# x by way of a bf16 copy in DRAM, one h matmul ahead at accumulator swaps, new round counts: a fused convolution and ELU layer on one core

## The chip, the cores and the metric

One core of a Trainium2 chip. The metric is the device time of one execution in microseconds. The kernel before took 740.35 us (median of 3 runs, 740.33 to 741.36). Every run also comes with the span of its core and the mean granted TensorE clock.

## The reference

A softmax-weighted causal convolution over 7 tokens (8 heads of 24 channels), then two matrix products with an ELU between them:

```python
def _attn_ref(x, weight):                 # x: 8 x 4096 x 192, weight: 8 x 7
    w = exp(weight - max(weight, -1)); w = w / (sum(w, -1) + 1e-09)
    x_pad = concatenate([zeros((B, 6, D)), x], axis=1)
    # ... windows of 7 tokens, one weight row per head
    return einsum('hk,bskhg->bshg', w, x_unf).reshape(B, S, D)

def _moe_ref(x, w_in, w_out):             # 32768 x 192, 192 x 2048, 2048 x 192
    h = x @ w_in
    g = np.where(h > 0.0, h, exp(np.minimum(h, 0.0)) - 1.0)
    return g @ w_out
```

## The kernel before

The tokens go in 32 supers of 1024 tokens, each super in 16 slots of 128 hidden features. TensorE is used as two row tiles of 64 partitions, each with 512 of a super's tokens for h. One h matmul chain (three of 512 columns) fills one of six PSUM banks. ACT takes exp of it, POOL clamps, DVE makes the ELU from both; then the bank is free. The products g times w_out of the super before are spread over the slots by `ROUNDS`. An accumulator is filled by one tile first and by the other afterwards, and each such swap is a semaphore wait. The next super's convolution also runs on PE. Its order against the rest comes from a modelled start time of each operation:

```python
LAG = -4
ROUNDS = (
    ((0, (0, 17)), (1, (6, 4, 7, 11, 4)), (0, (15,))),
    ((0, (0, 14, 8, 10)), (1, (4, 10, 5, 13))),
)
CONV_AT = ((2, 1, 1, 0), (8, 1, 1, 1), (12, 2, 0, 0), (15, 2, 0, 1))
EARLY_CONV = ((6, 1, 0, 0), (7, 1, 0, 1), (8, 1, 1, 0), (9, 1, 1, 1), (11, 2, 0, 0), (12, 2, 0, 1))
M_NS, R_NS, C_NS = 216, 83, 236
X_AT = ((3, 2, 1), (8, 2, 0), (11, 3, 2))
X_LATE = (17, 3, 2)
# ...
    # the schedule: one list of operations per row tile, merged by a modelled start time
    steps = []
    tiles, at = ([], []), [0, 0]

    def put(rt, ops_of):
        cost = {"h": M_NS, "o": R_NS, "c": C_NS, "w": M_NS}
        for op in ops_of:
            tiles[rt].append((at[rt], rt, len(tiles[rt]), op))
            at[rt] += cost[op[0]]
    for n in range(NP):
        s, i = divmod(n, NQ)
        convs = [(ahead, g, b) for at, ahead, g, b in EARLY_CONV if at == n]
        convs += [
            (s + ahead, g, b)
            for at, ahead, g, b in CONV_AT
            if at == i and s + ahead < NS
            and (s + ahead, g, b) not in [e[1:] for e in EARLY_CONV]
        ]
        for u in range(2):
            rt = 1 - u
            beside = [("c", 2 * cs + g - 2, b, u) for cs, g, b in convs]
            if n < first_round:
                beside += [("w", rt)] * WARM[1]
            beside += [single(item, rt) for item in rounds_at.get(n, ())]
            put(u, [("h", n, u, j) for j in range(3)])
            put(rt, beside)
        if n % 2:
            at[:] = [max(at)] * 2
    steps.extend(op for *_, op in sorted(tiles[0] + tiles[1], key=lambda v: v[:3]))
# ...  POOL: x by two casting DMAs a super, clamps
            def load_x(s, part):
                # ...
                src = bass.AP(
                    tensor=x_flat.tensor,
                    offset=row * D,
                    ap=[[D, P], [TOK * D, whole], [1, D]],
                )
                g.dma_start(xg[:, b, v0 : v0 + whole, :], src).then_inc(s_x[b][part - 1], 16)
                for at, ahead, part in X_AT:
                    if at == i and s and s + ahead < NS:
                        load_x(s + ahead, part)
                if n == X_LATE[0]:
                    load_x(*X_LATE[1:])
                for u in range(2):
                    W(s_exp, 2 * n + u + 1)
                    g.tensor_scalar(
                        out=E[:, n % NE, u, :],
                        in0=E[:, n % NE, u, :],
                        scalar1=1.0,
                        scalar2=0.0,
                        op0=ALU.min,
                        op1=ALU.max,
                    ).then_inc(s_clp)
# ...  DVE: the convolution's weights reversed, then the ELUs
            W(s_band, 48)
            v.tensor_copy(Tm[:], Tr[:, :, ::-1]).then_inc(s_tm)
                    W(s_clp, 2 * n + u + 1)
                    v.scalar_tensor_tensor(
                        out=gT[:, s % NG3, q, u, :],
                        in0=E[:, n % NE, u, :],
                        scalar=1.0,
                        in1=bank_of(op[:3]),
                        op0=ALU.subtract,
                        op1=ALU.max,
                    ).then_inc(s_tt)
# ...  PE: a chunk of h, and a product
                elif op[0] == "h":
                    _, n, r, j = op
                    s, q = divmod(n, NQ)
                    if n == 0:
                        W(s_ha, 2)
                        W(s_hd, 2)
                    if j == 0:
                        if Q_PART[q] < 3:
                            W(s_w[Q_PART[q]], 32)
                        else:
                            W(s_wc, 16)
                        W(s_att[s % 2], 16 * ((s + 1) // 2))
                        wait_bank()
                    ins = pe.matmul(
                        bank_of(op[:3]),
                        w_in[
                            HP * r : HP * (r + 1),
                            j,
                            2 * FC * (q // 2) + q % 2 : 2 * FC * (q // 2 + 1) : 2,
                        ],
                        att[HP * r : HP * (r + 1), s % 2, j, 0:GS],
                        start=(j == 0),
                        stop=(j == 2),
                        tile_position=(HP * r, 0),
                    )
                    if j == 2:
                        ins.then_inc(s_h[r])
                else:
                    # ...
                    W(s_tt, 2 * (NQ * t + q) + g + 1)
                    at_end = acc[:2] == (last, 1)
                    if x_ in begins:
                        if at_end:
                            wait_bank()
                        elif acc in previous:
                            taken(W, previous[acc])
                    elif steps[seen[acc]][2] != rt:
                        W(s_swap[1 - rt], ends_run[seen[acc]])
                    to = bank_of(("l",) + acc) if at_end else ops[:, g, :]
                    d0 = 0 if at_end else D * kb
                    t0 = 2 * P * half + P * kb
                    ins = pe.matmul(
                        to[:, d0 : d0 + D],
                        gT[HP * rt : HP * (rt + 1), t % NG3, q, g, t0 : t0 + P],
                        w_out[HP * rt : HP * (rt + 1), q, :],
                        start=(x_ in begins),
                        stop=(x_ in stops),
                        tile_position=(HP * rt, 0),
                    )
                    if x_ in ends_run:
                        ins.then_inc(s_swap[rt])
```

At the start, the first super's convolution runs as matmuls against diagonal weights (the head), into `att`. The weights of the later convolutions pass through DRAM (`conv_taps`), land in `Tr`, and the DVE copy shown above turns them into `Tm`. Filler matmuls on zeros (`WARM`) keep PE at work while there are no products.

## Time and profile before

| kernel before | us |
|---|---|
| median of 3 runs | 740.35 |
| span of the traced run | 739.3 |
| start to the first h of super 1 | 34.4 |
| one steady super | 22.36 |

The prediction below shows the profile's lines. They are read in this way. The first line of the page says how full each engine is. The windows table gives busy time over one super. The waits view says which instruction waited for which, how long in all, how often, and the longest time. A timeline line has the start and the length in us, engine, line, operation and what it writes and reads, how many in a row, and in brackets the idle time before it and what ended that.

### The profile page before, as it was taken

The numbers are of one execution on the slowest core, as the hardware profiler recorded it, in microseconds if no ns is written. First come the engines' busy times: TensorE is split into PE (matmuls) and PEld (weight loads), VectorE is DVE, ScalarE is ACT, GpSimd is POOL, SyncE is SP. The second block draws the span as 40 slices with busy tenths as digits, with TensorE's granted clock in tenths as the row PEclk, the third lists the DMA queues.
The fourth block names the chain that finished last, engine by engine and source line by source line (L and its number), as shares of the span: only waits on it lengthen the run. The fifth ranks groups of instructions, "written<-read, shape, count | busy, mean of one in ns | idle before, by whom it ended". The sixth has DMA issues, their size and how long they took to land.

```text
span 739.3 us, 28636 instructions
## 1 busy us (share of the span) xinstructions
PE 730.8 (99%) x11878; PEld 648.1 (88%) x11878; DVE 649.3 (88%) x1044; ACT 665.9 (90%) x1286; POOL 666.7 (90%) x1108
## 2 busy tenths in 40 slices
PE   8999999999999999999999999999999999999998
PEld 4589889999889999889899899998899998888987
DVE  4889889889889889889898898898898898898995
ACT  5889999999999999999999999999999999999984
POOL 7899999999999999999999999999999999998884
PEclk9999999999999999999999999999999999999999
DMA  9553444634434534546534435434445344343212
GB/s 171 93 95 74 72 78 77 96 73 79 74 65 91 94 71 69 88 60 96 89 67 71 88 67 95 80 75 71 77 79 95 72 80 75 72 82 82 56 36 67
DMA packets 131862, 58.97 MB, mean 80 GB/s; under 512 B 96020, under 2 KB 131348, under 8 KB 131732
## 3 DMA queue, kind: packets, MB, share of 16 engines
q0 software_dynamic: 43136, 17.28, 22.5%
q1 hardware_dynamic: 88308, 39.37, 20.8%
q8 instruction: 93, 1.52, 0.9%
q10 hardware_dynamic: 288, 0.49, 0.2%
q14 instruction: 37, 0.30, 0.1%
HBM read 35.61 MB, written 25.17 MB: 82 GB/s over the span
## 4 chain that ended last, share of the span: by engine, by line
PE 95%; DVE 2%; POOL 1%; ACT 1%; DMA 1%; issue 0%; SPq 0%; ACTq 0%
PE ops L759 49%; PE H L727 42%; PE H L703 2%; DVE gT L588 2%; POOL E L447 1%; PE H L759 1%; ACT E L519 1%; DMA xf<-in_x_dram 1%; PE H L660 0%; PE ops L660 0%; PE H L640 0%; DVE xh L554 0%; ACT csb L497 0%; POOL xg L397 0%; PE H L628 0%
## 5 line engine op out<-in xcount | busy, mean ns | idle before, releaser
L588 DVE SCALAR_TENSOR_TENSOR gT<-E,H 128x512 f16<-128x512 f32 x1024 | 642.6, 683 | 74.4 <-POOL E L447 69.0
L447 POOL TENSOR_SCALAR E<-E 128x512 f32<-128x512 f32 x1024 | 606.8, 614 | 60.9 <-ACT E L519 50.4
L727 PE MATMUL H<-att,w_in 64*128 64x512 bf16 x3072 | 626.2, 376 | 1.4 <-DVE gT L588 0.6
L519 ACT ACTIVATE E<-H 128x512 f32<-128x512 f32 x1024 | 573.4, 605 | 52.0 <-PE H L727 42.0
L759 PE MATMUL ops<-w_out,gT 64*128 64x192 f16 x8064 | 619.1, 243 | 0.6
L759 PEld LDWEIGHTS ops<-w_out,gT 64*128 64x128 f16 x8064 | 537.1, 94 | 41.0 <-PE ops L759 24.9
L727 PEld LDWEIGHTS H<-att,w_in 64*128 64x128 bf16 x3072 | 259.1, 94 | 29.0 <-DVE gT L588 7.9
L703 PE MATMUL H<-xg,Tm 64*128 64x240 bf16 x496 | 90.7, 263 | 0.9 <-DVE gT L588 0.9
L497 ACT ACTIVATE csb<-H 128x480 bf16<-128x480 f32 x124 | 71.3, 575 | 0.0
L489 ACT ACTIVATE osb<-ops 128x384 f32<-128x384 f32 x125 | 61.0, 488 | 10.2 <-PE ops L759 5.9
L397 POOL DMA_DIRECT2D xg<-in_x_dram x62 | 55.0, 888 | 0.1
L703 PEld LDWEIGHTS H<-xg,Tm 64*128 64x128 bf16 x496 | 43.4, 94 | 11.2 <-issue 1.1
L677 PE MATMUL ops<-zw 64*128 64x512 bf16 x24 | 8.8, 377 | 0.0
L759 PE MATMUL H<-w_out,gT 64*128 64x192 f16 x128 | 6.6, 243 | 0.0
L759 PEld LDWEIGHTS H<-w_out,gT 64*128 64x128 f16 x128 | 6.0, 94 | 0.0
L616 PE MATMUL ops<-zw 128*128 128x512 bf16 x9 | 4.0, 631 | 1.3 <-DVE zw L529 1.3
L402 POOL DMA_DIRECT2D w_in<-in_moe_w_in_dram x7 | 4.6, 662 | 0.3 <-DMA wh<-in_weight_dram 0.3
L580 DVE COPY osb<-ops 128x384 f32<-128x384 f32 x1 | 0.6, 557 | 4.5 <-PE ops L759 4.5
L616 PEld LDWEIGHTS ops<-zw 128*128 128x128 bf16 x9 | 1.2, 142 | 3.2 <-issue 1.9
L565 DVE CAST att<-H 128x512 bf16<-128x512 f32 x1 | 0.7, 693 | 2.3 <-PE H L660 2.3
L677 PEld LDWEIGHTS ops<-zw 64*128 64x128 bf16 x24 | 2.3, 94 | 0.5
L554 DVE CAST xh<-xf 128x768 bf16<-128x768 f32 x1 | 1.0, 995 | 1.9 <-DMA xf<-in_x_dram 1.9
(46 smaller groups left out, 26.2 us busy)
## 6 DMA issues: line engine op xcount, KB each, us to landing
out_dram<-osb SPq DMA_DIRECT2D x126, 192.0 KB, 3.7
xg<-in_x_dram POOLq DMA_DIRECT2D x61, 240.0 KB, 5.2
w_in<-in_moe_w_in_dram POOLq DMA_DIRECT2D x4, 192.0 KB, 6.2
w_out<-in_moe_w_out_dram POOLq DMA_DIRECT2D x1, 768.0 KB, 15.0
att<-csb SPq DMA_TRANSPOSE x31, 3.5
xf<-in_x_dram ACTq DMA_DIRECT2D x1, 384.0 KB, 3.1
xf<-in_x_dram SPq DMA_DIRECT2D x1, 384.0 KB, 4.2
w_in<-in_moe_w_in_dram POOLq DMA_DIRECT2D x1, 288.0 KB, 10.3
```

The lines of the kernel that those rows point to most:

```text
L397: g.dma_start(xg[:, b, v0 : v0 + whole, :], src).then_inc(s_x[b][part - 1], 16)
L402: g.dma_start(w_in[HP * r : HP * (r + 1), :, c0:c1], moe_w_in.rearrange("(p j) f -> p j f", j=3)[:, :, c0:c1],).then_inc(s_w[k], 16)
L447: g.tensor_scalar(out=E[:, n % NE, u, :], in0=E[:, n % NE, u, :], scalar1=1.0, scalar2=0.0, op0=ALU.min, op1=ALU.max,).then_inc(s_clp)
L489: a.activation(*out_pieces(acc), ACT.Copy).then_inc(s_oev)
L497: return a.activation(csb[:, s % 2, :].rearrange("p (j v h i) -> p h j v i", j=3, v=2 * WPG, h=HEADS)[:, h0 : h0 + HB], bank_of(("c", m, b ...
L519: a.activation(E[:, n % NE, u, :], bank_of(op[:3]), ACT.Exp).then_inc(s_exp)
L588: v.scalar_tensor_tensor(out=gT[:, s % NG3, q, u, :], in0=E[:, n % NE, u, :], scalar=1.0, in1=bank_of(op[:3]), op0=ALU.subtract, op1=ALU.m ...
L616: pe.matmul(ops[:, 0, :], zw[:, 0:P], zw[:], start=True, stop=True)
L677: pe.matmul(ops[:, rt, :], zw[HP * rt : HP * (rt + 1), 0:P], zw[HP * rt : HP * (rt + 1), :], start=True, stop=True, tile_position=(HP * rt ...
L703: ins = pe.matmul(bank_of(op[:3])[:, n1 * hh : n1 * (hh + 1)], Tm[HP * rt : HP * (rt + 1), h, :], xg[HP * rt : HP * (rt + 1), s % NXB, :, ...
L727: ins = pe.matmul(bank_of(op[:3]), w_in[HP * r : HP * (r + 1), j, 2 * FC * (q // 2) + q % 2 : 2 * FC * (q // 2 + 1) : 2,], att[HP * r : HP ...
L759: ins = pe.matmul(to[:, d0 : d0 + D], gT[HP * rt : HP * (rt + 1), t % NG3, q, g, t0 : t0 + P], w_out[HP * rt : HP * (rt + 1), q, :], start ...
```

## The change

The intent is threefold. PE should not idle at the three swaps of a super: the first h of the slot goes ahead of the product that must wait. POOL should have fewer DMAs to issue: it casts a whole super of x into a DRAM copy with one DMA, and SyncE loads from there. And the head should let the first h start sooner. The counts of products per slot, the slots of the convolution, and its order (now by single chunks) change with it. So does a load of w_in: POOL now issues both halves of the last piece (8 issues in place of 7), where SyncE copied the second half from the first. Core of the diff, cuts marked by "...", three comments added:

```diff
-    ((0, (0, 17)), (1, (6, 4, 7, 11, 4)), (0, (15,))),
-    ((0, (0, 14, 8, 10)), (1, (4, 10, 5, 13))),
+    ((0, (0, 20)), (1, (1, 7, 9, 7, 8)), (0, (12,))),
+    ((0, (0, 15, 7, 10)), (1, (5, 8, 6, 13))),
...
-CONV_AT = ((2, 1, 1, 0), (8, 1, 1, 1), (12, 2, 0, 0), (15, 2, 0, 1))
+CONV_AT = ((4, 1, 1, 0), (10, 1, 1, 1), (12, 2, 0, 0), (15, 2, 0, 1))
...
-M_NS, R_NS, C_NS = 216, 83, 236
+M_NS, R_NS, C_NS = 215.8, 82.5, 102.5
...
-X_AT = ((3, 2, 1), (8, 2, 0), (11, 3, 2))
-X_LATE = (17, 3, 2)
+X_PAD, X_COPY, X_LOAD = 8, 1, 15
+X_LATE = (13, 22)
...
+    turns_at = {
+        n
+        for n, items in rounds_at.items()
+        if items
+        and rounds_at.get(n - 1)
+        and rounds_at[n - 1][-1][:2] == items[0][:2]
+        and rounds_at[n - 1][-1][4] != items[0][4]
+    }
...
-            beside = [("c", 2 * cs + g - 2, b, u) for cs, g, b in convs]
+            beside = [
+                ("c", 2 * cs + g - 2, b, u, hh)
+                for cs, g, b in convs
+                for hh in range(HB)
+            ]
...
-            put(u, [("h", n, u, j) for j in range(3)])
+            if rt and n in turns_at:
+                beside.insert(0, ("h", n, 1, 0))
+            put(u, [("h", n, u, j) for j in range(u and n in turns_at, 3)])
...
+    xb = nc.dram_tensor("x_cast", (NT, D), BF16).ap()
...
-            return H[:, (0, 2, 0)[j], GS * r : GS * r + GS // 2]
+            return H[:, (0, 2, 1)[j], GS * r : GS * r + GS // 2]
...
+            def copy_x(s):                                   # POOL, in slot X_COPY
+                W(s_cv, 4 * (s - NXB - 1) + 1)
...
+                g.dma_start(
+                    xb[s * SUP : (s + 1) * SUP, :].rearrange("(p t) d -> p (t d)", p=P),
+                    x_flat[s * SUP : (s + 1) * SUP, :].rearrange("(p t) d -> p (t d)", p=P),
+                ).then_inc(s_xb[s % 2], 16)
...
             W(s_xha, 1)                                      # PE, the halo matmuls
-            W(s_xh, 1)
...
             ins.then_inc(s_tp)
+            W(s_xh, 1)
...
                     if n == 0:
-                        W(s_ha, 2)
-                        W(s_hd, 2)
+                        W(s_ha, (1, 1, 2)[j])
+                        W(s_hd, (0, 1, 2)[j])
...
+            def load_cast(s):                                # SyncE, in slot X_LOAD
+                W(s_cv, 4 * (s - NXB))
+                W(s_xb[s % 2], 16 * ((s - 1) // 2 + (s % 2)))
...
+                for part in range(2):
+                    row = s * SUP + GS * part - PAD
+                    for w0, w1, rows in ((0, WPG - 1, P), (WPG - 1, WPG, GS - TOK * (WPG - 1) + PAD)):
+                        v0 = WPG * part
+                        sy.dma_start(
+                            xg[0:rows, s % NXB, v0 + w0 : v0 + w1, :],
+                            bass.AP(tensor=xb.tensor, ...),
+                        ).then_inc(s_xq[s % NXB][part], 16)
```

## The prediction

> **What bounds the kernel now.** Some names first. A super is 1024 tokens (32 of them), a slot is one of its 16 chunks of 128 hidden features. In a slot each of the two row tiles of TensorE (partitions 0-63 and 64-127) does three h matmuls (x times w_in, 512 columns), then or before them a number of products (g times w_out, 192 columns), and in four slots of a super two chunks of the next convolution (240 columns). h goes through ACT (exp), POOL (clamp) and DVE (ELU) before its PSUM bank is free; six banks rotate. I read the page first, for the engine that is full.
>
> ```profile
> PE 730.8 (99%) x11878; PEld 648.1 (88%) x11878; DVE 649.3 (88%) x1044; ACT 665.9 (90%) x1286; POOL 666.7 (90%) x1108
> ...
> L588 DVE SCALAR_TENSOR_TENSOR gT<-E,H 128x512 f16<-128x512 f32 x1024 | 642.6, 683 | 74.4 <-POOL E L447 69.0
> L447 POOL TENSOR_SCALAR E<-E 128x512 f32<-128x512 f32 x1024 | 606.8, 614 | 60.9 <-ACT E L519 50.4
> L727 PE MATMUL H<-att,w_in 64*128 64x512 bf16 x3072 | 626.2, 376 | 1.4 <-DVE gT L588 0.6
> ...
> L759 PE MATMUL ops<-w_out,gT 64*128 64x192 f16 x8064 | 619.1, 243 | 0.6
> L759 PEld LDWEIGHTS ops<-w_out,gT 64*128 64x128 f16 x8064 | 537.1, 94 | 41.0 <-PE ops L759 24.9
> ...
> L703 PE MATMUL H<-xg,Tm 64*128 64x240 bf16 x496 | 90.7, 263 | 0.9 <-DVE gT L588 0.9
> ```
>
> Everything is near 90%, PE is at 99%, and the chain that ended last is 95% PE. But busy PE hides a tile that idles beside the other. So next I matched the trace's matmuls to the two tiles in program order. Starts that follow each other on one tile are 216 ns apart for h, 82.5 for a product and 102.5 for a convolution chunk. Per super and tile that is 48 x 216 + 128 x 82.5 + 8 x 102.5 = 21.75 us. The starts of successive supers are 22.36 us apart (the two table rows below, over one super each), so each tile idles 0.61 us per super, some 19 us in all. That, and the start, is all there is to win on PE.
>
> ```profile
> core 0: us, PE busy (x) PEld busy (x) DVE busy (x) ACT busy (x) POOL busy (x), PEclk, DMA share, GB/s
> 392.75:415.11 22.36, 22.34 (x373) 20.20 (x369) 20.06 (x33) 20.72 (x41) 20.62 (x35) 1.00 0.43 79
> 415.11:437.47 22.36, 22.34 (x372) 20.22 (x370) 20.15 (x33) 20.72 (x41) 20.79 (x36) 1.00 0.43 79
> ```
>
> The view of waits, and PE's timeline at one of them, say where it lies:
>
> ```profile
> PEld ops L759 <- PE ops L759: 24.9, 94, 0.5
> ```
> ```profile
> 412.42 0.38 PE L727 MATMUL H<-att,w_in 64*128 64x512 bf16 x1
> 412.44 0.24 PE L759 MATMUL ops<-w_out,gT 64*128 64x192 f16 x1
> 412.52 0.39 PE L727 MATMUL H<-att,w_in 64*128 64x512 bf16 x1
> 412.90 0.25 PE L759 MATMUL ops<-w_out,gT 64*128 64x192 f16 x1
> 412.91 0.39 PE L727 MATMUL H<-att,w_in 64*128 64x512 bf16 x1
> ```
>
> 94 is three per super for 31 supers and one more: the swaps, where an accumulator passes from one tile to the other. At 412.42 tile 1 streams its last h (until 412.64), at 412.44 tile 0 its last product. Tile 1's next product, on tile 0's accumulator, starts at 412.90: 263 ns after its h. Tile 0's second h, behind it in the queue, starts at 412.91, 175 ns late. In a steady super I find 263 twice, and 58 at the third swap, where two convolution chunks (205 ns) stand ahead: 263 - 205 = 58. With some 12 ns behind each, tile 1's 0.61 us is complete. Tile 0 loses as much: twice 185, 141 on an eviction at the first product of half 1, and 80.
>
> **What the Trainium skill says.** "TensorE: Matmul & The Clock Gate", Part 3, has matmuls in strict program order at start and end, with only weight loads pulled ahead. The trace agrees: tile 0's free h waits behind tile 1's blocked product, and all swaps are released at the same distance from the h before (its 376 ns end plus about 100), even where tile 0's product had finished earlier. "DMA: Bandwidth & Descriptors", SWDGE vs HWDGE vs iDMA, says that a casting DMA must come from GpSimd; so the cast stays there and only the plain load can go to SyncE. "Perfetto Trace Analysis", DMA Instruction — SWDGE (GPSIMD), says that such a row is descriptor generation, not movement; here it holds POOL for 0.89 us while landing takes 5.2, and POOL's clamps wait behind it:
>
> ```profile
> 398.00 0.61 POOL L447 TENSOR_SCALAR E<-E 128x512 f32<-128x512 f32 x1 [0.28 <-ACT E L519]
> 398.56 0.89 POOL L397 DMA_DIRECT2D xg<-in_x_dram  x1
> 399.49 3.02 POOL L447 TENSOR_SCALAR E<-E 128x512 f32<-128x512 f32 x5
> ```
>
> **The change part by part.**
> *An h ahead at swaps.* The matmul put ahead covers 216 of 263 ns, so 47 remain. Swaps one and two gain 216 each, the third (convolutions are moved off it) 58 - 47 = 11. That is 443 ns per super, x 31 + 216 = 13.95 us. Tile 0 is no longer blocked, as its second h is issued before the product.
> *Convolution from slots 2 and 8 to 4 and 10.* Slot 4 has no products; it grows from 648 to 853 ns, so the first product of half 1 on tile 0 comes 1501 ns after the accumulator's end instead of 1296. The 141 ns wait needed 1437 and goes. It lay beside tile 1's losses, so I add nothing.
> *Head.* The halo matmuls stop waiting for DVE's cast of the second half (they started at 6.57; the ACT half was done at 4.81), some 0.4 us. The first h waits only for the first piece of att; the third starts when att's last piece is there, 0.43 us sooner. Together 0.8 us. The start is then a chain of ACT, POOL and DVE, which shifts as a whole:
>
> ```profile
> 12.19 0.38 ACT L484 ACTIVATE att<-H 128x256 bf16<-128x256 f32 x1 [1.16 <-PE H L660]
> ...
> 12.72 0.37 PE L727 MATMUL H<-att,w_in 64*128 64x512 bf16 x1 [0.57 <-ACT att L484]
> ```
>
> *x by way of DRAM.* POOL issues one DMA per super instead of two of 0.89 us. The w_in loads (192 runs) held it 0.63 us, x (640 runs) 0.89; a copy of 128 rows I estimate from these at 0.62, with the step to the next clamp 0.65. POOL was never the bound, so the 1.1 us saved per super is worth nothing by itself, except where it ended a wait: about 0.4 us near 656, where a pad, a remainder load and x stood together. SyncE's loads have from slot 15 to slot 12 of the next super, 18 us; x landed in 5. Hidden, as is the doubled traffic at a DMA share of 0.43.
> *Finer convolution order, exact durations.* Ordering only: 0.
>
> Sum: 740.35 - 13.95 - 0.8 - 0.4 = 725.2 us, if nothing else becomes the wait.
>
> **The rivals.**
> *First: the copy in slot 1 delays a bank.* From the end of an h to the reuse of its bank, an undisturbed chain takes 197 (to exp) + 678 (to clamp) + 646 (to ELU) + 683 (its time) + 58 = 2262 ns; spacings in a queue are 494 on ACT, 576 on POOL, 605 on DVE. These I checked on the 398 us event above, where they give each start within 10 ns. In the new counts slots 1, 2 and 3 take 1225, 1308 and 1638 + 59. From the start of slot 1: the last clamp of slot 0 starts at about 0.95, the copy at 1.51, and the clamps of (1,0), (1,1), (2,0) at 2.16, 2.73, 3.31 us. The ELUs follow at 2.80, 3.41, 4.01, the last ends at 4.70 and frees its bank at 4.76. Tile 1's h of slot 4, six bank turns later because the convolution now takes one there, wants it at 1225 + 1308 + 1697 + 205 = 4.435. So PE would wait 0.3 us in each of 28 supers, 8.4 us. Without the copy the bank is free 0.3 before. For it: the arithmetic, and that a DMA row blocks POOL. Against it: in the kernel before, both loads stand just before long slots (15 and 13 products), and the tightest bank turns have 58 to 70 ns, which is no wait; whoever set these counts did so on such waits, and would hardly accept a new one where a later slot was free.
> *Second: short slots 14 and 15.* Slot 15's end comes 789 + 1430 = 2219 ns after the last h of slot 13, whose bank the first h of the next super takes after 2262: about 45 ns, x 30 = 1.4 us.
> *Third: another engine becomes the bound.* Per super: DVE 32 x 605 = 19.4 us, POOL 32 x 576 + 0.65 = 19.1, ACT 32 x 494 + 4 x 450 + 4 x 370 = 19.1. All lie under 21.75, so no.
> *Fourth: the loads come late or disturb the transposes of att*, now started two slots later. About 6 us remain from the convolution's eviction to the next super; landings took 3.4 to 5.1. Not expected.
>
> **Range and chances.** With both stalls in full: 725.2 + 8.4 + 1.4 = 735.0. Without: 725.2. I give the stall 60%, as the arithmetic fits the old trace but the design speaks against it: 0.6 x 735.0 + 0.4 x 725.2 = 731.1, so 731. Eight times in ten between 724.5 and 737.5. Over 2% faster means below 725.5: only with no stall and nothing else lost, 0.17. Slower by 2%: 0.01. Within 2%: 0.82.
>
> **What would show it right or wrong.** PEld's wait for products should fall from 24.9 us to under 10, with the product one h and about 47 ns behind. Successive supers should start 21.95 us apart without the stall, 22.25 with it; the stall would show as PE waiting for DVE at the second tile's h of slot 4, right after POOL's copy. The first h should start near 11.9 us, the first exp near 12.75. I am wrong if POOL's copy is much shorter than 0.6 us, if the swaps keep their 263, if PE waits on x or att, or if the start is held by a weight load.

## The result, and the profile after

| | before | after |
|---|---|---|
| median of 4 runs, us | 740.45 | 738.83 |
| lowest to highest | 740.33 to 741.36 | 736.52 to 738.92 |
| first h of super 1 (traced run) | 34.39 | 34.65 |
| supers 1 to 30, together | 671.32 | 666.79 |
| one steady super | 22.36 | 22.25 |
| last part | 33.59 | 32.76 |

The ratio is 0.9968, with a 95% interval of 0.9947 to 0.9989: the same within 2%. A ratio here is always the mean time of one kernel's fast runs over that of the other's in the same rounds, so it is not quite the ratio of the medians. 738.83 lies above the predicted range of 724.5 to 737.5.

One thing must be seen first. Of the four runs, the traced one had 736.52 us (span 734.2, clock 1.000), and the three others 738.81 to 738.92 (spans 736.4 to 736.5, clock 0.998). The trace shows the quicker kind.

From the page after: the engines, and POOL's copies.

```profile
PE 726.9 (99%) x11878; PEld 653.8 (89%) x11878; DVE 655.4 (89%) x1044; ACT 675.9 (92%) x1286; POOL 637.4 (87%) x1080
...
L410 POOL DMA_DIRECT2D x_cast<-in_x_dram x29 | 15.4, 530 | 0.0
```

PE is still at 99%. POOL lost 29 us of work: 62 issues of x (55.0 us) became 29 copies (15.4) and 4 loads of the first supers (3.9); some came back, as the clamps took 611.1 us in place of 606.8. Over two supers, the windows table after:

```profile
390.94:413.19 22.25, 22.24 (x369) 20.32 (x369) 20.30 (x33) 21.08 (x41) 19.59 (x34) 1.00 0.39 95
413.19:435.45 22.26, 22.25 (x369) 20.28 (x369) 20.35 (x33) 21.08 (x41) 19.71 (x35) 1.00 0.37 89
```

A super takes 22.25 us, just what the prediction gave for the branch with the stall, and 0.50 us above the streaming time of 21.75. The waits view after says where these 0.50 us lie:

```profile
PEld ops L771 <- PE ops L771: 16.5, 92, 0.2
PEld H L739 <- DVE gT L605: 14.5, 44, 0.7
PEld H L739 <- issue: 9.6, 31, 0.4
```

The product's wait for the other tile has shrunk from 0.5 us at most to 0.2. The second line had 7.9 us in 21 waits before (shown with the swap experiment below), the third 0.7 us in 2. They are h that waits for a bank, at two places of each super. The first is slot 4, in the second line. POOL's timeline around slot 1, and PE's and its weight loads' at slot 4:

```profile
414.23 1.86 POOL L464 TENSOR_SCALAR E<-E 128x512 f32<-128x512 f32 x3 [0.16 <-ACT E L536]
416.04 0.53 POOL L410 DMA_DIRECT2D x_cast<-in_x_dram  x1
```
```profile
418.83 0.37 PE L717 MATMUL H<-xg,Tm 64*128 64x240 bf16 x2
419.20 0.82 PE L739 MATMUL H<-att,w_in 64*128 64x512 bf16 x5
```
```profile
419.19 0.33 PEld L739 LDWEIGHTS H<-att,w_in 64*128 64x128 bf16 x5 [0.27 <-DVE gT L605]
```

The copy sits between clamps of slot 1. Some 3 us later two convolution chunks of tile 1 start, at 418.83 and 102.5 ns after it; its h could follow at 419.04. It starts at 419.20, and what released its weight load is DVE's ELU. So tile 1 loses 0.17 us here, and tile 0, queued behind, 0.24. The second place is the first h of the next super, on tile 0, after the short slots 14 and 15: the third line, whose releaser the view doesn't name. This h starts 147 ns after the ELU that frees its bank. It is 264 ns late, where it was 80 before (beside tile 1's losses), and tile 1's product, queued behind it, loses 147. Matching the trace's matmuls to the program order gives, for tile 1 in one steady super:

| idle of tile 1, ns | before | after |
|---|---|---|
| swap at slots 14 and 3 | 263, 263 | 47, 47 |
| swap at slot 8 | 58 | 46 |
| slot 4, bank | - | 168 |
| product behind the next super's first h | - | 147 |
| some 10 behind each | about 30 | about 42 |
| sum | about 610 | about 500 |

The start, in the slots where the early convolutions run, got slower. PE's timeline before, and then after, at slot 12:

```profile
28.90 0.39 PE L727 MATMUL H<-att,w_in 64*128 64x512 bf16 x1
29.00 0.26 PE L703 MATMUL H<-xg,Tm 64*128 64x240 bf16 x1
29.49 0.60 PE L727 MATMUL H<-att,w_in 64*128 64x512 bf16 x3 [0.20 <-DVE gT L588]
```
```profile
28.94 0.38 PE L717 MATMUL H<-xg,Tm 64*128 64x240 bf16 x2 [0.21 <-DVE gT L605]
29.54 0.82 PE L739 MATMUL H<-att,w_in 64*128 64x512 bf16 x5 [0.22 <-DVE gT L605]
```

Before, an h of tile 0 (28.90) got through between the chunks (28.89 and 29.00); after, none does, and all h start only at 29.54. From slot 6 to slot 13 the kernel before takes 10.82 us, the changed one 11.86.

### The profile page after: what moved, and what is told of

It reads as the page before. It is cut to its first block, busy times and chain, and to the rows that moved or that the text cites. A ratio compares the mean times of both kernels' runs of the same rounds, so it can differ in the third digit from the quotient of the medians.

```text
span 734.2 us, 28751 instructions
## 1 busy us (share of the span) xinstructions
PE 726.9 (99%) x11878; PEld 653.8 (89%) x11878; DVE 655.4 (89%) x1044; ACT 675.9 (92%) x1286; POOL 637.4 (87%) x1080
## 4 chain that ended last, share of the span: by engine, by line
PE 95%; DVE 2%; POOL 1%; ACT 1%; issue 1%; ACTq 0%
PE ops L771 49%; PE H L739 41%; PE H L717 3%; DVE gT L605 2%; POOL E L464 1%; PE H L771 1%; PE ops L633 1%; ACT E L536 0%; PE H L677 0%; PE ops L677 0%; PE H L657 0%; ACT csb L514 0%; POOL x_cast L410 0%; PE H L644 0%; POOL x_cast L407 0%
## 5 line engine op out<-in xcount | busy, mean ns | idle before, releaser
L605 DVE SCALAR_TENSOR_TENSOR gT<-E,H 128x512 f16<-128x512 f32 x1024 | 649.1, 683 | 63.4 <-POOL E L464 53.0
L464 POOL TENSOR_SCALAR E<-E 128x512 f32<-128x512 f32 x1024 | 611.1, 616 | 85.5 <-ACT E L536 80.0
L739 PE MATMUL H<-att,w_in 64*128 64x512 bf16 x3072 | 633.2, 376 | 1.7 <-DVE gT L605 1.2
L536 ACT ACTIVATE E<-H 128x512 f32<-128x512 f32 x1024 | 587.4, 603 | 40.1 <-PE H L739 24.6
L771 PEld LDWEIGHTS ops<-w_out,gT 64*128 64x128 f16 x8064 | 538.8, 94 | 18.4 <-PE ops L771 16.5
L717 PEld LDWEIGHTS H<-xg,Tm 64*128 64x128 bf16 x496 | 45.4, 93 | 15.9 <-issue 1.3
L410 POOL DMA_DIRECT2D x_cast<-in_x_dram x29 | 15.4, 530 | 0.0
L391 POOL DMA_DIRECT2D xg<-in_x_dram x4 | 3.9, 982 | 0.0
L677 PE MATMUL H<-xT,Dg 64*128 64x256 bf16 x32 | 2.6, 326 | 0.0
```

Of the source, the lines that this page charges most:

```text
L410: g.dma_start(xb[s * SUP : (s + 1) * SUP, :].rearrange("(p t) d -> p (t d)", p=P), x_flat[s * SUP : (s + 1) * SUP, :].rearrange("(p t) d - ...
L464: g.tensor_scalar(out=E[:, n % NE, u, :], in0=E[:, n % NE, u, :], scalar1=1.0, scalar2=0.0, op0=ALU.min, op1=ALU.max,).then_inc(s_clp)
L536: a.activation(E[:, n % NE, u, :], bank_of(op[:3]), ACT.Exp).then_inc(s_exp)
L605: v.scalar_tensor_tensor(out=gT[:, s % NG3, q, u, :], in0=E[:, n % NE, u, :], scalar=1.0, in1=bank_of(op[:3]), op0=ALU.subtract, op1=ALU.m ...
L717: ins = pe.matmul(bank_of(op[:3])[:, n1 * hh : n1 * (hh + 1)], Tm[HP * rt : HP * (rt + 1), h, :], xg[HP * rt : HP * (rt + 1), s % NXB, :, ...
L739: ins = pe.matmul(bank_of(op[:3]), w_in[HP * r : HP * (r + 1), j, 2 * FC * (q // 2) + q % 2 : 2 * FC * (q // 2 + 1) : 2,], att[HP * r : HP ...
```

## The experiments

Theory A: in the steady state the gain of the swaps goes back into two bank waits, one from POOL's copy in slot 1, one from the short slots 14 and 15. Rivals: the way of x through DRAM costs something by itself, or the swaps are not the cost. Theory B: at the start the convolution's new cost in the modelled order (102.5, so 205 for a pair, in place of 236) makes the difference. What makes some runs 2.3 us slower was open at first; theory C came last. Chips differ a little, so each result stands beside the kernel before on the same chip.

### The changed kernel once more, on another chip

No edit.

> The changed kernel once more, nothing edited. Its profiled run had a span of 734.2 us at a granted clock of 1.0; its three other runs 736.4 to 736.5 us at 0.998. If the 2.3 us between them come from the clock alone (a clock released one step later at the start in some executions), then every run at 0.998 lies within 0.3 us of 738.8 and every run at 1.0 within 0.3 us of 736.5, and a trace at 0.998 shows the same steady supers of 22.25 us and all of the difference before super 1 starts (34.65 us). The rival: the difference is spread over the supers (a wait that comes and goes), and runs between the two values occur.

735.75 us (735.32 to 736.92, 5 runs) against 740.76; ratio 0.9936 (0.9923 to 0.9948). The steady super is 22.25 us again, but super 1 starts at 33.58 us, not 34.65. So the kernel doesn't always take 738.8, and what varies lies in the first 35 us. The clock alone doesn't sort the runs: one at 0.998 took 736.92 us, not 738.8, and those at 1.000 took 735.32 to 736.61.

### The copy of x in slot 5

```diff
-X_PAD, X_COPY, X_LOAD = 8, 1, 15
+X_PAD, X_COPY, X_LOAD = 8, 5, 15
```

> POOL's copy of x stands before the first clamp of slot 5 instead of slot 1, nothing else. Copy theory: the wait of 0.17 to 0.24 us at the second tile's h of slot 4 goes, supers start 22.07 us apart instead of 22.25 (as the one full super without a copy did in the changed kernel, 22.07), 28 times, so 5.1 us less: about 733.7 us for runs like the 738.8 ones. Rival (the short slot 4 alone, with its convolution and two evictions on ACT, makes the bank late): supers stay at 22.2 or more and the time above 737.

731.26 us (730.41 to 733.68); ratio 0.9876 (0.986 to 0.9893). One steady super in the windows table, and the waits view's line for the banks:

```profile
409.01:431.08 22.07, 22.07 (x371) 20.14 (x368) 20.18 (x33) 20.72 (x41) 19.65 (x35) 1.00 0.40 97
```
```profile
PEld H L739 <- DVE gT L605: 7.5, 16, 1.4
```

The super falls by 0.18 us, and the wait for banks by 28 waits (44 to 16) and 7.0 us, one per copy. The stall of slot 4 is the copy's. The whole time fell by 4.5 us on this chip; the expected 733.7 was reckoned from the first chip's 738.83.

### The counts of slots 14 to 2 as well

```diff
-    ((0, (0, 20)), (1, (1, 7, 9, 7, 8)), (0, (12,))),
+    ((0, (0, 20)), (1, (2, 8, 8, 7, 7)), (0, (12,))),
-X_PAD, X_COPY, X_LOAD = 8, 1, 15
+X_PAD, X_COPY, X_LOAD = 8, 5, 15
```

> The copy before slot 5 as in the run above, and the counts 1, 7, 9, 7, 8 of the second stretch turned into 2, 8, 8, 7, 7: slots 14 and 15 grow by 82 ns each. Short-slot theory: the first h of each super waits 147 ns for the bank of slot 13's second h, as 2219 ns lie between and 2354 are needed; with 2384 the wait goes, supers go from 22.07 to 21.92 and the time from 731.3 to 726.6 us. Rival (that wait is for the att of the super, not for the bank): no change, 731.

726.14 us (726.09 to 726.23) against 740.05; ratio 0.9806 (0.9793 to 0.982). One steady super:

```profile
406.72:428.63 21.91, 21.91 (x369) 20.05 (x368) 20.09 (x33) 20.73 (x42) 19.56 (x35) 1.00 0.43 105
```

With two products in slot 14 and eight in slot 15, tile 1 no longer loses anything at the start of a super. Tile 0's first h still waits there, 176 ns in place of 334, but that lies beside tile 1's swaps and costs nothing. What tile 1 has left above 21.75 us is three times some 47 ns at the swaps. Theory A holds in size and place: 22.25, 22.07, 21.91.

### The swaps alone, in the kernel before

```diff
+    turns_at = { ... }                      # as in the change
...
-            put(u, [("h", n, u, j) for j in range(3)])
+            if rt and n in turns_at:
+                beside.insert(0, ("h", n, 1, 0))
+            put(u, [("h", n, u, j) for j in range(u and n in turns_at, 3)])
```

> The kernel before with one part of the change alone: the first h of tile 1 put ahead of the products at the three swaps. Counts, convolution slots, x path and head as before. Swap theory by itself: two swaps go from 263 to 47 ns, the third from 58 to nothing, 0.50 us per super, 15 us in all: 725. Bank theory: six bank turns in the kernel before have only 58 to 70 ns to spare, which is no reserve, so part of it comes back as waits on DVE at the h of slots 0 to 4 and 12 to 14; then supers of about 22.0 us and 729 to 735 us.

753.41 us (753.23 to 754.87) against 740.76; ratio 1.0174 (1.0161 to 1.0188). It is 12.7 us slower: both theories missed. The waits view of the kernel before, that of this kernel, and PE's timeline of this kernel at slot 3:

```profile
PEld H L727 <- DVE gT L588: 7.9, 21, 0.6
```
```profile
PEld H L737 <- DVE gT L598: 36.0, 76, 1.2
```
```profile
403.76 0.38 PE L737 MATMUL H<-att,w_in 64*128 64x512 bf16 x1
404.32 0.39 PE L737 MATMUL H<-att,w_in 64*128 64x512 bf16 x2 [0.19 <-DVE gT L598]
```

Tile 1 does a slot's products before its h. The h put ahead thus wants its bank earlier by the time of all those products, 15 x 82.5 = 1238 ns in slot 3, and the bank isn't free: tile 1 idles 435 ns in slot 3, 477 in slot 14 and 83 in slot 8, in place of 263, 263 and 58. A super takes 22.79 us. An early h doesn't only fill a wait, it moves a bank's deadline. The change's new counts are there to make this work, not a detail beside it.

### The changed kernel without an h ahead

```diff
+    turns_at = set()
```

> The changed kernel without the h ahead at the swaps; its counts, convolution slots and x path stay. Swap theory: all three swaps cost 263 and about 12 ns again instead of 47 and 10, so 0.65 us more per super; the copy's wait in slot 4 (0.17 to 0.24) goes, as PE comes 0.22 us later to it. Supers of about 22.70 us instead of 22.25, and the time near 735.8 + 31 x 0.45 = 750 us. Rival (the h ahead is worth little, as it was a loss of 12.7 us put into the kernel before): within 3 us of 735.8.

746.24 us (746.07 to 746.52) against 740.05; ratio 1.0078 (1.0064 to 1.0092). A super takes 22.57 us. The waits view:

```profile
PEld ops L772 <- PE ops L772: 32.3, 94, 0.5
PEld H L740 <- DVE gT L606: 7.9, 16, 1.7
```

All three swaps now cost 263 ns each, as the new slots have no convolution ahead of the third. The two bank waits cost tile 1 next to nothing now, hidden behind the slower PE. This is why 750 us was expected and 746 came: taking one wait away uncovers another, and putting it back covers that again. The h ahead is worth 22.57 - 22.25 = 0.32 us per super within the changed kernel. Three swaps at 47 in place of 263 would be 0.65; the bank waits take back half of it. (The prediction's 0.44 was counted on the old slots, with only two swaps of 263.)

### The way of x alone

```diff
# the changed kernel with the old counts, the old slots of the convolution,
# the copy in slot 3, and turns_at empty
-M_NS, R_NS, C_NS = 215.8, 82.5, 102.5
+M_NS, R_NS, C_NS = 215.8, 82.5, 118
```

> The x path, the head and the weight load of the change alone: no h ahead at swaps, the counts, convolution slots and convolution order of the kernel before, the copy before slot 3, where a load of x stood. If POOL's saved time is worth nothing by itself: supers of 22.35 us as before (22.36), and 738 to 741 us, what differs being the start and the clock at the start. Rival (a POOL freed of 1.1 us per super shortens bank waits that the kernel before has): supers under 22.25 and under 737 us.

741.43 us (739.07 to 742.63) against 740.05; ratio 1.0009 (0.9988 to 1.003), a super 22.355 us. Two runs at clock 1.000 had 739.07 and 740.29, two at 0.998 some 742.6. So in the old schedule fewer DMAs on POOL are worth nothing, and the DRAM detour costs nothing.

### The old way of x with the good counts

```diff
# the kernel before with turns_at and the h ahead, convolution in slots 4 and 10, and
+    ((0, (0, 20)), (1, (2, 8, 8, 7, 7)), (0, (12,))),
+    ((0, (0, 15, 7, 10)), (1, (5, 8, 6, 13))),
```

> The kernel before with the h ahead at swaps, the convolution slots of the change and the counts of the 726.15 us run, but x loaded as before: two DMAs of POOL of 0.9 us per super, before slots 3 and 11. If the x path itself is worth nothing (as by itself it was): 726 to 727.5 us. If POOL's time matters once PE is faster: the DMA before slot 11 delays the clamp of the first h of slot 12, whose bank the h ahead of slot 14 takes with only some 30 ns to spare, by 0.3 us; supers of 22.15 to 22.2 us and 733 to 735 us.

732.30 us (732.13 to 732.59) against 740.97; ratio 0.9882 (0.9868 to 0.9897), a super 22.07 us, with a bank wait of 208 ns at slot 14's early h (the two issues of 0.89 us stand in slots 3 and 11). That lies between the two forecasts. With the same counts and x by way of DRAM it was 726.1 on another chip, with supers of 21.91. So once PE is quicker, the same detour that was worth nothing is worth 0.16 us per super, some 5 us; the rest may be the old head, which this kernel keeps, and the chip.

### Two h ahead

```diff
-                beside.insert(0, ("h", n, 1, 0))
-            put(u, [("h", n, u, j) for j in range(u and n in turns_at, 3)])
+                beside[:0] = [("h", n, 1, 0), ("h", n, 1, 1)]
+            put(u, [("h", n, u, j) for j in range(2 * (u and n in turns_at), 3)])
# and the copy in slot 5, the counts 2, 8, 8, 7, 7, two fillers, cost 118
```

> As the last, with two h matmuls (432 ns) ahead of the products at each swap instead of one (216). Swap theory: 432 is over 263, so the 47 and 10 ns left at each swap go, 0.165 us per super; supers of 21.75 to 21.78 us and about 720.5 us. Rival (PE then comes too early to banks, as in the kernel before with swaps alone): part or all of it returns as waits on DVE, 722 to 727 us.

728.86 us (727.2 to 729.54) against 740.97; ratio 0.9828 (0.981 to 0.9846). The 47 ns at the swaps are gone, but bank waits of 173 ns (slot 8) and 180 ns (the next super's first h) take their place, and a super takes 21.995 us. The rival was right: the bank is the next limit.

### The start: the order, more fillers, the old head

The cost of a convolution chunk in the modelled order, back to half of the old 236:

```diff
-M_NS, R_NS, C_NS = 215.8, 82.5, 102.5
+M_NS, R_NS, C_NS = 215.8, 82.5, 118
```

> A convolution chunk is put in the program order as if it took 118 ns (so two take 236, as in the kernel before) instead of 102.5. Nothing else. Order theory: in the slots with a convolution the free second h of tile 0 comes ahead of tile 1's first h, which waits for its bank, again; the start gets back the 1.0 us that it lost between slots 6 and 13, super 1 starts near 33.6 us instead of 34.65, and the time is 1 us less, 737.8; the steady supers gain at most 0.05 us each, so not below 736. Rival (the start is held by DVE and ACT in any order, or by the copy of slot 13): no change within 0.3 us.

737.87 us (737.29 to 738.18) against 740.76; ratio 0.9959 (0.9944 to 0.9974). By its time it is slower than the changed kernel on the same chip (735.75). But slots 6 to 13 take 10.84 us, as before the change, in place of 11.86. The two starts are not of one kind, though. Like with like it is 11.05 against 11.86 in quick starts (11.05 in the kernel of x alone and in the last one below, which both have 118) and 10.84 against 11.61 in slow ones. So theory B is right, with 0.8 us in place of 1.0. What masks it is another loss: all four runs had a clock of 0.995 to 0.998, and the trace shows the granted clock at half from 17.13 to 20.54 us.

Two filler matmuls a slot, to keep the clock up:

```diff
-WARM = (9, 1)
+WARM = (9, 2)
```

> The changed kernel with two filler matmuls per slot and tile instead of one in the twelve slots at the start that have no products. Clock theory: the runs that are slower are those in which the clock falls back to half for one stretch of 3.4 us between 12 and 30 us, because PE is only some 72% streaming there (864 of 1196 ns per slot); with 1080 of 1196 it is not thrown back, all runs show 1.0 or what a later release alone gives (0.999), and the spread of 735.3 to 736.9 (and 738.9) shrinks to about 735 to 736. Rival (the fallback comes from the head before 12 us, where nothing is changed): some of the runs still show 0.998 or less. The steady supers stay at 22.25.

734.71 us (734.67 to 734.81, five runs, all at clock 1.000) against 740.05; ratio 0.9922 (0.9909 to 0.9936). It looked like a cure. Both edits together say that it isn't:

> The changed kernel with two fillers per slot at the start (which kept the clock in all five runs, 734.71 us) and with convolution chunks put in as 118 ns. Order theory, now with the clock out of the way: 0.7 to 1.0 us less from the start, 733.7 to 734.0 us, super 1 starts near 32.1 us instead of 32.95, steady supers as before at 22.24. Rival: 734.7, no change.

737.85 us against 740.97; ratio 0.9945 (0.9922 to 0.9969): three runs at a clock of 0.997 to 0.998, one clean one of 734.42. The trace has the half clock from 17.11 to 20.53 us.

All parts together (copy in slot 5, counts, two fillers, cost 118):

> All that helped together: the copy in slot 5, the counts 2, 8, 8, 7, 7, two fillers and the order of 118 ns. If they add up: 726.15 less 0.6 to 1.0 for the start, about 725.3 us, every run at a clock of 1.0, supers of 21.91 us. If the order pays only in the slots that wait for a bank, no more than 0.3 us are gained against 726.15.

726.07 us (725.27 to 728.75) against 740.97; ratio 0.9804 (0.9782 to 0.9826). Two clean runs of 725.27 and 725.51; the traced one of 728.75 has the half clock again.

The kernel before, the changed kernel and the changed kernel with the old head, on one chip:

> The kernel before, unedited, for a second trace of its start. Its first trace had the clock released at 10.13 us, its first h at 12.72 and super 1 at 34.39 us in a span of 739.3; most of its timed runs have spans of 737.4 to 738.7. If an early release alone makes that difference, this trace shows the release at 4 to 6 us, the first h near 11.6 and super 1 near 33.3, supers of 22.36 as ever. Then the changed kernel (super 1 at 33.58 with an early release) gained nothing at the start with the clock alike. If the trace again shows 34.4 with an early release, the changed start did gain 0.8 us.

> The changed kernel again, as control of the next run, on whatever chip this is. Clock theory: runs at 1.0 or 0.999 lie at 735.3 to 736.7, runs at 0.998 or less 1.2 to 2.4 us above them, and between one in five and three in four of the runs are of the second kind. Steady supers of 22.25 us in either kind of trace.

> The changed kernel with the head of the kernel before (halo matmuls after both casts, the third piece in the bank of the first, the first h after all of att). If the new head is worth its 0.8 us: 0.8 us more than the control in runs of like clock, first h 1.1 us later and first exp 0.8 us later. If the head's gain is lost in the chain of the start (slots 6 to 13): within 0.3 us of the control. If the new head is what makes the clock fall back: no run at 0.998 or less here, while the control has some.

The kernel before: 741.43 us in one run (clock 0.997; its trace has the clock at half from 7.74 to 11.15 us, in the head, and so has the old head in the changed kernel, from 7.97 to 11.38). The changed kernel: 736.34 us (735.43 to 738.86, 6 runs; ratio 0.994, 0.9927 to 0.9953), two of its runs at 738.58 and 738.86 (the traced one). With the old head (its waits and its bank as before): 737.24 us (736.36 to 737.43; ratio 0.9947, 0.9935 to 0.9959), about 1 us more than the changed kernel's other four, so by the runs the new head is worth about its predicted 0.8. The traces say where it may come from only in part. Where the clock came late (the first traces of both kernels, 10.1 and 10.5 us), the first exp is at 13.56 us before and 12.77 after. The trace of the old head here can't be laid beside one with the new head, since its clock fell back in the head; nor does the second trace of the kernel before decide its question (super 1 at 34.43 us, but with the clock fallen back). This time the changed kernel's trace was one of the slow kind (span 736.5, clock 0.998), the first that could be laid beside the quick one: super 1 starts at 37.08 us against 34.65 and 33.58, all supers after it are alike.

### Why some starts are slow: a DVE copy against POOL's clamps

The windows table of that slow execution, and the same stretch of the quick trace of the run on another chip, which also had its full clock early (PE's busy time is the second number, the clock the third from the end):

```profile
7.20:17.43 10.23, 6.44 (x82) 4.03 (x80) 6.83 (x7) 4.65 (x10) 8.60 (x13) 1.00 1.16 169
17.44:20.84 3.40, 3.40 (x18) 1.34 (x18) 3.40 (x6) 2.13 (x4) 1.73 (x3) 0.50 1.43 194
```
```profile
7.20:17.43 10.23, 9.10 (x96) 4.63 (x93) 6.33 (x12) 6.64 (x14) 10.22 (x16) 1.00 1.20 176
17.44:20.84 3.40, 3.00 (x25) 1.22 (x24) 3.38 (x6) 2.44 (x6) 2.76 (x6) 1.00 1.46 194
```

The clock is at half for 3.40 us, but PE idled for 3.8 us of the stretch before that, against 1.1 in the quick trace. The timelines of DVE and POOL in the slow execution, and DVE's copy in the first trace of the changed kernel, say why:

```profile
12.26 3.83 DVE L591 COPY Tm<-Tr 128x1024 bf16<-128x1024 bf16 x1 [1.61 <-DMA Tr<-conv_taps]
16.02 3.07 DVE L605 SCALAR_TENSOR_TENSOR gT<-E,H 128x512 f16<-128x512 f32 x5
```
```profile
12.30 3.50 POOL L464 TENSOR_SCALAR E<-E 128x512 f32<-128x512 f32 x6
18.63 0.61 POOL L464 TENSOR_SCALAR E<-E 128x512 f32<-128x512 f32 x1 [2.82 <-ACT E L536]
```
```profile
12.19 0.55 DVE L591 COPY Tm<-Tr 128x1024 bf16<-128x1024 bf16 x1
```

A copy of 0.43 to 0.55 us took 3.83. It ended, at 16.09, when POOL's six clamps in a row were through (15.80) and POOL had nothing left: all six banks were taken, since the ELUs that free them stand behind the copy. Only then did the ELUs start, at 16.02 in place of about 13.0. The Trainium skill, "SBUF — State Buffer", section "Who interferes with whom", says that a DVE copy in a two-port mode and a GpSimd instruction contend for a shared port pair, and that the one that issues second "fully blocks" until the other has finished. That fits; no view names the port or the mode. The traces add that the loser can wait through six clamps in succession, and that in three of them it was the copy whose recorded start came first, by 0.04 to 0.10 us.

The traces of all kernels agree. Where the copy starts 0.14 us or more ahead of POOL's first clamp, it takes 0.42 to 0.78 us. Where it starts between 0.1 us ahead and 0.6 us after it, seven traces, it took 3.89, 3.83, 3.83, 3.47 and 2.70 us, and twice got in between two clamps (0.87 and 0.51). In the five traces with the old head they don't meet: the copy is 0.51 to 1.72 us ahead (in the first of them at 12.72 us, the clamp at 14.26). That they can't is not shown. The copy waits for a DMA, which landed between 11.2 and 12.9 us over all traces (at 12.70 in that one), and where the clock came early the old head's first clamp is at 12.31 and 12.49 us.

With the new head and an early clock the first clamp is at 12.16 to 12.67 us, hardly sooner, though the first exp has ended by 11.34 to 11.81. What holds it is POOL's own queue: in these traces the clamp starts within 0.01 us of the end of POOL's last DMA issue of the start, that of w_out. With the old way of x that issue ended at 11.50 to 11.76 us; the change puts one more issue (w_in, 0.64 us) ahead of it. So POOL's clamps begin about when the copy's DMA lands, and then follow each other without a gap. When PE gets its full clock is read from the spacing of its matmuls (512 columns: 427 ns before and 216 after; 256 columns: 213 and 109); it varies from 4.0 to 10.5 us. In the first trace of the changed kernel it was 10.5 us, so the clamp came at 13.47, and the copy was out of the way.

Theory C: the copy causes the slow start, and the half clock follows from PE's idling. Rival: the clock falls back by itself. Three kernels, one chip. The copy on ACT, behind the sixth exp:

```diff
-            W(s_band, 48)
-            v.tensor_copy(Tm[:], Tr[:, :, ::-1]).then_inc(s_tm)
...
                     ).then_inc(s_exp)
+                    if (n, u) == (2, 1):
+                        W(s_band, 48)
+                        a.activation(Tm[:], Tr[:, :, ::-1], ACT.Copy).then_inc(s_tm)
```

> The changed kernel with one edit: the copy that reverses the convolution's weights (Tm from Tr, 128x1024 bf16) goes from DVE to ACT, behind the sixth exp. New theory, from reading the start of all traces again: in the five executions whose start is slow (the changed kernel's second trace and three others by 2.3 us, a fifth by less) this DVE copy takes 2.7 to 3.9 us, in all others 0.42 to 0.87. It begins there while POOL's clamps run, first one at 12.2 us, and ends when POOL has run out of clamps; DVE's ELUs stand behind it, so the banks stay taken, PE idles through nearly a whole 3.41 us stretch (0.47 to 0.89 us busy), and only then the granted clock falls to a half for 3.41 us. So the fallback is a consequence. With the copy on ACT there is nothing on DVE to lose against POOL: every run between 734.3 and 737.0 us, none at 738 or more, the trace without a stretch at half clock after the first release, steady super 22.25 us. Rival: the clock falls back by itself when it is released near 7 us; then a third or more of the runs stay at 738.5 to 739, clock 0.995 to 0.998, as in the six runs of the changed kernel on the chip before (two of six) and the four of the first (three of four). Second rival: the copy on ACT (about 1 us) sits in front of the exps and costs as much; then all runs near 736.5 to 737.

735.38 us (735.02 to 736.15, all five at a clock of 0.999 or 1.000) against 740.75; ratio 0.9928 (0.9916 to 0.9941). No slow run. That alone is no more than the five clean runs with two fillers were, and the unedited changed kernel wasn't run on this chip; the next two runs, on the same chip, add to it. The copy in ACT's timeline:

```profile
15.17 1.10 ACT L541 ACTIVATE Tm<-Tr 128x1024 bf16<-128x1024 bf16 x1
```

The copy on DVE, but made to wait for POOL's first clamp, so that it always meets them:

```diff
             W(s_band, 48)
+            W(s_clp, 1)
             v.tensor_copy(Tm[:], Tr[:, :, ::-1]).then_inc(s_tm)
```

> The changed kernel with one wait more: DVE's copy of the convolution's weights waits for POOL's first clamp, so it always arrives while POOL's second clamp runs. Theory of the copy against the clamps: the slow start becomes the usual case; the copy takes over 2 us in the trace, most runs 738 to 739.5 us at a clock of 0.995 to 0.998, whatever the chip, provided that the copy loses at the next change of clamps too, which it did in five of seven traces in which it began inside a clamp. If it wins there, it takes 0.8 to 1.0 us and the run 735 to 736.5. Rival, the clock's own fallback: the copy takes 0.43 to 0.9 us, the runs spread as without the wait (a third to three quarters at 738.5 and more), and half-clock stretches appear also in traces with a short copy.

738.12 us (736.63 to 738.3, all four at a clock of 0.998) against 740.75; ratio 0.996 (0.9946 to 0.9974). Three runs of four are slow, as the theory has it. The trace fell on the fourth (736.63), and there the copy got in after 0.76 us:

```profile
13.02 0.76 DVE L592 COPY Tm<-Tr 128x1024 bf16<-128x1024 bf16 x1 [2.61 <-POOL E L464]
```

Even so the ELUs began 0.7 us later than they could have, PE idled 1.54 us, and the half clock followed, from 16.04 to 19.45 us. So in all five traces with a fallback after 12 us, PE had idled just before. But idling alone doesn't decide: the kernel with two h ahead idled more (PE busy 1.54 us from 14.24 to 17.65, here 1.87 from 12.63 to 16.04) and kept its clock. It also shows what costs the time. Its copy took 2.70 us, and its super 1 started at 35.04 us, against 32.95 with two fillers and a copy of 0.43: some 2 us late without any fallback. That the three slow runs here had the long copy is argued from their times, not seen. And all together with the copy on ACT:

```diff
-    ((0, (0, 20)), (1, (1, 7, 9, 7, 8)), (0, (12,))),
+    ((0, (0, 20)), (1, (2, 8, 8, 7, 7)), (0, (12,))),
-M_NS, R_NS, C_NS = 215.8, 82.5, 102.5
+M_NS, R_NS, C_NS = 215.8, 82.5, 118
-X_PAD, X_COPY, X_LOAD = 8, 1, 15
+X_PAD, X_COPY, X_LOAD = 8, 5, 15
# and the copy of Tm on ACT
```

> All that helped in one kernel: the copy of x in slot 5, the counts 2, 8, 8, 7, 7, the old program order at the start (a convolution chunk counted as 118), and the weights' copy on ACT. Theory of the copy: every run between 724.6 and 726.0 us, as the two clean runs of the kernel with two fillers had 725.27 and 725.51, and none at 728 or more; steady super 21.91 us; faster than the kernel before by 2.0 to 2.2%, faster than the changed one by 1.5%. Rival: one run in three at 728 to 729 as before.

724.94 us (724.88 to 725.38, five runs, all at clock 1.000) against 740.75; ratio 0.9786 (0.9773 to 0.98): the best version, and the only one over 2% faster than the kernel before. It is 1.4% under the changed kernel with the copy on ACT on the same chip (means 725.02 and 735.43). A super takes 21.91 us. Its trace is the plainest case for theory C: the copy's DMA landed at 12.91 us, 0.24 us after the first clamp (12.67), and yet the first ELU started at 13.35 and super 1 at 33.26. Ten runs on this chip with the copy on ACT have no slow one, and three of four with the copy on DVE made to meet the clamps do.

## Why the prediction was right or wrong

**The sizes of the steady state were right.** "Successive supers should start 21.95 us apart without the stall, 22.25 with it": 22.25 came. The swap's residue was 46 to 47 ns, as worked out. The super's time fell short of its gain for the reason of the first rival, POOL's copy and the bank of slot 4's second h, and moving the copy alone removed that. Two sizes were off and cancelled. The copy took 0.53 us, not 0.62, and its stall is worth 0.18 us per super, not 0.3. The short slots cost tile 1 147 ns per super, not 45: a super's first h starts 147 ns after its bank's release, in the kernel before too, where the 2262 ns count on the 58 of the other h. Why it is 147 there is not shown; in the program that h alone has a second wait, for att. ACT, POOL and DVE didn't become the bound, the loads were hidden, and x by way of DRAM was worth nothing by itself. PEld's wait for products fell to 16.5 us, not under 10, as 92 waits of some 0.18 us remain: the view counts how long the weight load waits, not the 47 ns that PE loses. And one reading was too strong: that the trace agrees with Part 3 on matmuls in strict program order. It agrees that a free h waits behind a blocked product. But matched to the program, 3244 of the 11784 matmuls of the kernel before start over 20 ns, up to 196 ns, before one of the other tile that the program puts ahead of them.

**The first step that failed is in "Range and chances": "the design speaks against it".** The arithmetic gave 735.0 us for the branch with both stalls; I gave it 60%, because "whoever set these counts did so on such waits, and would hardly accept a new one". The trace's arithmetic deserved more than a guess about an author. That cost 735.0 - 731.0 = 4.0 us.

**The second is "Ordering only: 0".** The finer order isn't neutral where a chunk of the one tile is blocked on a bank: in slot 12, with a pair of chunks at 205, tile 1's blocked h comes ahead of tile 0's second, free one (at 216) in the order; with 236 it came after it. (In the slots with a filler it is tile 0's third.) 0.8 us, by the traces.

**The third, which took the result out of the range, is of the head: "The start is then a chain of ACT, POOL and DVE, which shifts as a whole".** It doesn't. The first exp came at 12.77 us against the predicted 12.75 in the first trace, where the clock came late. But POOL's queue holds its issues of the start, one more than before, so that with an early clock the first clamp stays at 12.16 to 12.67 us; and DVE's queue holds a copy that waits for a DMA and doesn't shift, and the clamps meet it. I had looked at POOL's DMAs as what blocks a queue in the steady part only, and at no DVE instruction at all. It costs some 2.3 us in the executions where it happens: three of the four recorded ones by their spans and clocks, 736.4 to 736.5 us at 0.998, as in the traced slow one on chip 5.

The sum: 735.0 + 0.8 + 2.3 = 738.1 us, against 738.83; 0.7 us remain. It is no closer than that, since the 2.3 are counted from the first trace, whose clock came late; from the quick trace on another chip super 1 is 37.08 - 33.58 = 3.5 us later. Leaving the runs with slow starts out, the changed kernel took 735.32 to 736.92 us on three chips, inside the range and 0.5 to 0.7% under the kernel before. So the steady part was forecast by working it out, and 60% against 40% was the guess; that the range was missed hung on a collision that a run may or may not have.

**What the intent came to.** 13.95 us were to be won at the swaps. 4.5 came in the steady part, and the rest went back into two bank waits; with the copy in slot 5 and two numbers of the counts moved, another 9.6 us came (the ratio went from 0.9936 to 0.9806).

## What to carry to other kernels

An instruction put ahead to fill a wait also takes its buffer ahead; check the deadline of that buffer for the whole time that it moved, as the same edit without new counts was 12.7 us slower. When a stretch gets earlier, look for what in the neighbour queues does not get earlier with it (here a copy that hangs on a DMA, and POOL's own DMA issues), since the two may now meet. And when a small clock loss varies from run to run, look at what PE waited for just before it, and compare a quick and a slow trace of the same kernel before blaming the clock.

## What the Trainium skill lacked or had wrong

- "SBUF — State Buffer", Who interferes with whom: it says that the second to issue blocks for the other's whole instruction. The runs show more: a DVE copy of 0.43 us lost to six POOL clamps in a row, one every 0.58 us, and took 3.83 us (3.47 to 3.89 in three more traces), until POOL had run dry; in another it got in after the fifth (2.70), in two after the first (0.51, 0.87). The page lets the one that issues first have the ports; in three of these traces the copy's recorded start was 0.04 to 0.10 us ahead of the first clamp's, and it lost.
- "TensorE: Matmul & The Clock Gate", Part 1: it tells of a window of 3413 ns, and of idling for a whole one before the clock falls. Here a stretch of 3.41 us at half clock followed such stretches in which PE was still busy for 0.47 to 0.89 us, one with 1.87 us, and in the head of two traces 2.03 and 2.08 us; another with 1.54 us (with two fillers a slot) was followed by none. How much work is enough stays open. The full clock first came between 4.0 and 10.5 us (by the matmuls' spacing) in kernels with nearly the same start.
- "Perfetto Trace Analysis", DMA Instruction — SWDGE (GPSIMD): it has no figure for how long the issue holds POOL. Measured means: 0.53 us for a contiguous DRAM-to-DRAM cast of a super, 0.66 for w_in, 0.89 for half a super of x (640 runs of 384 bytes as stored).
- No page has what the runs show of bank reuse: an h that waited starts 58 ns after the end of the ELU that frees its bank (its weight load at 53), and 147 ns (weight load at 116) where it is the first of a super.
